# Routing tokens to expert blocks: a table written by expert and rank during attention, in place of a one-hot inversion between the stages

## The chip, the cores and the metric

The kernel runs on one core of a Trainium2 chip. The metric is the device time of one execution in microseconds; lower is better. The engines named below are TensorE (PE in the profile, with its weight loads as PEld), VectorE (DVE), ScalarE (ACT), GpSimd (POOL) and SyncE (SP). SP and POOL issue the DMAs here, each through a queue of its own, onto the same 16 DMA engines.

## The reference

Two stages follow one another. The first is attention in chunks of 64 positions; the second sends each token to one of eight experts by the cosine between the token and the expert's embedding.

```
q, k, v: (8, 8, 576, 64) fp32        # batch, heads, positions, head size
per batch, head and chunk of 64 positions:
    scores = q_c @ k_c.T / 8
    attn   = exp(scores - rowmax);  attn /= attn.sum + 1e-9
    out    = attn @ v_c
x = out as (4608, 512)               # a row is a token, all heads side by side

xn     = x / (norm(x) + 1e-6);  en = emb / (norm(emb) + 1e-6)      # emb (8, 512)
logits = xn @ en.T / tau
e      = argmax(logits)              # the first one, where two are equal
gate   = softmax(logits)[e]
y      = gate * (relu(x @ w1[e]) @ w2[e])     # w1 (8, 512, 1024), w2 (8, 1024, 512)
```

## The kernel before

**Attention.** The 4608 tokens are 36 tiles of 128. A loop over `t` runs all steps of the stage in a staggered order that is written out by hand: in one turn `turn_a(t)`, `turn_qk(t + 3)`, the loads of a later tile, `logits(t - 2)`, `scores(t + 2)`, `turn_x(t - 1)`, `values(t)`, `weights(t + 2)` and `norm(t)`. Each engine takes its instructions in the order of the program text. Loads of q, k and v go through SP's queue (L110, L123). q and k have four buffers each and v has two. `values` writes a tile of x to the DRAM tensor `x_rows` through POOL's queue (L208), from one of three SBUF buffers. `norm` sums the squares of each row on ScalarE (L213). `logits` leaves eight numbers per token in PSUM (L227); they are not yet divided by the row's norm, which changes neither the order of the experts nor their argmax.

Behind the loads of the last tiles SP's queue carries the first experts' weights (L78): for expert 0 and for expert 7, two copies of w1 and one of w2, 2 MB each. A second copy of w2 comes when the SBUF of attention is free.

**The seam.** All routing is done between the stages, for all 36 tiles at once, at L286 to L485. VectorE finds each token's expert as a one-hot row `eq`. Two matmuls with a matrix of ones and a triangular one give each token's rank among the tokens of its expert. Each expert's tokens are cut into groups of 64 (G). Step `j` of the expert stage takes two groups at a time: group `j` counted from the front, with one set of weight buffers, and group `j` counted from the back, with the other. So a block is 128 rows for two experts, there are at most 40 (`NST`), and 37 are used with these inputs. `mid` is the number of blocks.

Each token thus knows its block and its row in it. The expert stage needs the reverse: for each block and row, the token. The kernel inverts the map with one-hot matrices: for each of the 36 tiles VectorE builds a 128 x 128 matrix `oh` of rows (L470), and TensorE multiplies it with columns of token number and gate per block, summed over the tiles in `inv` (L471). `src_row`, `dst_row` and `gate_at` are read from the sum (L481 to L485). The gates themselves are computed for all tokens at once with one Sqrt and one Exp (L445, L450).

**The expert stage.** `gather(j)` fetches the 128 rows of block `j` from `x_rows` by an indirect DMA on POOL's queue (L535). `turn_xb` transposes them (L549, copied by VectorE at L551). `hidden` is the first product (L561; relu on VectorE at L572 and on ScalarE at L570), `turn_h` transposes its result (L582; copies at L586 on VectorE and L584 on ScalarE), and `result` is the second product (L594). ScalarE multiplies by the gate (L602), and an indirect DMA on POOL's queue scatters the rows to the output (L603). Weights are loaded on SP's queue under a condition, only where a block's expert differs from the one two blocks before (L522). The loop over the first 36 blocks runs, per turn, `hidden(j+1)`, `turn_h(j)`, `turn_xb(j+2)`, `result(j-1)` and `gather(j+4)`. Blocks from 36 on run under a condition, one step after the other.

Of the kernel before, what the change touches and what calls it, by code (L numbers as in the profile page):

```python
# [21 lines left out]
NO_ROW = 200000.0  # L22
# [3 lines left out]
def kernel(  # L26
# [23 lines left out]
    scale = 1.0 / float(Dh) ** 0.5  # L50

    x_rows = nc.dram_tensor("x_rows", (N, D), FP32, kind="Internal").ap()

# [9 lines left out]
    lg = keep.tile([P, NT, E], FP32, name="lg")  # L63
    nsq = keep.tile([P, NT], FP32, name="nsq")
    src_row = keep.tile([P, NST], I32, name="src_row")
    dst_row = keep.tile([P, NST], I32, name="dst_row")
    gate_at = keep.tile([P, NST], FP32, name="gate_at")
    eblk = keep.tile([1, 2, NST], I32, name="eblk")
    fresh = keep.tile([1, 2, NST], I32, name="fresh")
    n_steps = keep.tile([1, 1], I32, name="n_steps")  # L70

# [10 lines left out]

    VW = 72
    with (
# [9 lines left out]
        lg_ps = ps_l.tile([P, NT, E], FP32, name="lg_ps")  # L94
# [4 lines left out]
        enT = one.tile([P, KD, E], FP32, name="enT")  # L99

# [110 lines left out]
        def norm(t):  # L211
            junk = one.tile([P, D], FP32, tag="junk", name="junk")
            nc.scalar.activation(junk, st[t]["x"], AF.Square, accum_out=nsq[:, t : t + 1])  # L213

# [9 lines left out]
        def logits(t):  # L224
            d = st.pop(t)
            for c in range(KD):
                nc.tensor.matmul(  # L227
                    lg_ps[:, t],
                    lhsT=d["xT"][:, c],
                    rhs=enT[:, c],  # L230
                    start=(c == 0),
                    stop=(c == KD - 1),
                )

# [22 lines left out]
        for t in range(-3, NT + 2):  # L257
# [11 lines left out]
            if 0 <= t - 2:  # L269
                logits(t - 2)  # L270
            if 0 <= t + 2 < NT:
                scores(t + 2)
            if 0 <= t - 1 < NT:
                turn_x(t - 1)
# [7 lines left out]
            if 0 <= t < NT:  # L282
                norm(t)
            if t == -2:
                set_up_experts()
        nc.vector.tensor_copy(lg, lg_ps)  # L286
# [10 lines left out]

    with (  # L300
        tc.tile_pool(name="seam", bufs=1) as sp,
        tc.tile_pool(name="hot", bufs=4) as hp,
        tc.tile_pool(name="ps_r", bufs=1, space=PSUM) as ps_r,
    ):
        onesb = sp.tile([P, P], BF16, name="onesb")
        sltb = sp.tile([P, P], BF16, name="sltb")
        io_i = sp.tile([P, P], I32, name="io_i")
        io = sp.tile([P, P], FP32, name="io")
        tok_i = sp.tile([P, NT], I32, name="tok_i")
        tok1 = sp.tile([P, NT], FP32, name="tok1")  # L310
        pref = sp.tile([P, E], FP32, name="pref")
        carry = sp.tile([P, E, NT], FP32, name="carry")
        nc.vector.memset(onesb, 1.0)
        make_upper_triangular(nc, sltb, val=1.0, diag=False)
        nc.gpsimd.iota(io_i, pattern=[[1, P]], base=0, channel_multiplier=0)
        nc.gpsimd.iota(tok_i, pattern=[[P, NT]], base=1, channel_multiplier=1)
        nc.vector.tensor_copy(io, io_i)
        nc.vector.tensor_copy(tok1, tok_i)
        nc.vector.tensor_scalar(pref, io[:, 0:E], -1.0, float(E), ALU.mult, ALU.add)
        nc.vector.memset(carry, 1.0)  # L320
        nc.vector.memset(carry[:, :, 0:1], 0.0)

        ES = [P, E, NT]
        SE = [P, NT, E]

        def by_e(ap):
            return ap.unsqueeze(2).to_broadcast(ES)

        def by_s(ap):
            return ap.unsqueeze(1).to_broadcast(ES)  # L330


        lmax = sp.tile([P, NT], FP32, name="lmax")
        sel = sp.tile(ES, FP32, name="sel")
        pm = sp.tile([P, NT], FP32, name="pm")
        eq = sp.tile(ES, FP32, name="eq")
        nc.vector.tensor_reduce(lmax, lg, axis=AX.X, op=ALU.max)
        nc.vector.tensor_tensor(sel, lg.rearrange("p s e -> p e s"), by_s(lmax), ALU.is_equal)
        nc.vector.tensor_tensor(sel, sel, by_e(pref), ALU.mult)
        nc.vector.tensor_reduce(pm, sel.rearrange("p e s -> p s e"), axis=AX.X, op=ALU.max)  # L340
        nc.vector.tensor_tensor(eq, sel, by_s(pm), ALU.is_equal)


        cum = sp.tile(ES, FP32, name="cum")
        eqb = sp.tile(ES, BF16, name="eqb")
        exb = sp.tile(ES, BF16, name="exb")
        totb = sp.tile([P, E], BF16, name="totb")
        nc.vector.tensor_tensor_scan(
            cum.rearrange("p e s -> p (e s)"),
            carry.rearrange("p e s -> p (e s)"),  # L350
            eq.rearrange("p e s -> p (e s)"),
            0.0,
            ALU.mult,
            ALU.add,
        )
        nc.vector.tensor_copy(eqb, eq)
        nc.vector.tensor_tensor(exb, cum, eq, ALU.subtract)
        nc.vector.tensor_copy(totb, cum[:, :, NT - 1])
        tot = ps_r.tile([P, E], FP32, name="tot")
        rank = ps_r.tile(ES, FP32, name="rank")  # L360
        nc.tensor.matmul(tot, lhsT=onesb, rhs=totb, start=True, stop=True)
        rank_f = rank.rearrange("p e s -> p (e s)")
        nc.tensor.matmul(
            rank_f, lhsT=onesb, rhs=exb.rearrange("p e s -> p (e s)"), start=True, stop=False
        )
        nc.tensor.matmul(
            rank_f, lhsT=sltb, rhs=eqb.rearrange("p e s -> p (e s)"), start=False, stop=True
        )


        nb = sp.tile([P, E], FP32, name="nb")
        first = sp.tile([P, E], FP32, name="first")
        off = sp.tile([P, E], FP32, name="off")
        ngm1 = sp.tile([P, 1], FP32, name="ngm1")
        mid = sp.tile([P, 1], FP32, name="mid")
        half = 0.5 - 0.5 / G
        nc.vector.tensor_scalar(nb, tot, 1.0 / G, half, ALU.mult, ALU.add)
        nc.vector.tensor_scalar(nb, nb, ROUND, ROUND, ALU.add, ALU.subtract)
        nc.vector.tensor_tensor_scan(first, carry[:, 0, 1 : E + 1], nb, 0.0, ALU.mult, ALU.add)
        nc.vector.tensor_scalar(ngm1, first[:, E - 1 : E], -1.0, None, ALU.add)  # L380
        nc.vector.tensor_scalar(mid, first[:, E - 1 : E], 0.5, 0.25, ALU.mult, ALU.add)
        nc.vector.tensor_scalar(mid, mid, ROUND, ROUND, ALU.add, ALU.subtract)
        nc.vector.tensor_tensor(first, first, nb, ALU.subtract)
        nc.vector.tensor_scalar(off, first, float(G), None, ALU.mult)


        JE = [1, 2 * NST, E]
        e_of = sp.tile([1, 2, NST], FP32, name="e_of")
        jj = sp.tile([1, 2, NST], FP32, name="jj")
        ge = sp.tile(JE, FP32, name="ge")  # L390
        nc.vector.tensor_copy(jj[:, 0], io[0:1, 0:NST])
# [294 lines left out]
```

## Time and profile before

| | |
|---|---|
| median of 3 runs | 822.38 us (820.01 to 822.48) |
| the profiled execution | 820.02 us, of which the span is 818.2 us |
| TensorE busy | 749.4 us, 92% of the span |
| VectorE busy | 217.9 us, 27% |
| ScalarE busy | 181.6 us, 22% |
| GpSimd busy | 101.9 us, 12% |
| DMA | 129.99 MB in 148726 packets, 115366 of them under 512 B |
| attention | start to the last logits at 183.0 us |
| seam | to the first transposes of the expert stage at 229.5 us |
| expert stage | 15.34 us per block in the loop, to the end |

The page cuts the span into 40 slices and gives the busy share of each engine in tenths; a 9 is 90% or more. PEclk is the granted clock of TensorE, in tenths. In a timeline each line has the start and the length in microseconds, the engine, the line of the program, the operation, what it writes and reads, and in brackets how long the engine had been idle and what ended that. "Chain" means the work that ended last, followed back from the end, at each step to what released it. Times "to landing" run from the issue of a DMA until its data have arrived.

### The profile page before, as it was taken

To read this page: it belongs to the slowest core of one execution; us is meant where nothing else is said; L and a number is where in the kernel's file an instruction comes from. 1 tells how busy PE (TensorE), PEld (TensorE's weight loads), DVE (VectorE), ACT (ScalarE), POOL (GpSimd) and SP (SyncE) were. 2 spreads that over 40 slices of the span, in tenths; PEclk is the share of its full clock that TensorE was granted. 3 is DMA by queue.
4 is the path that set the end of the run, shared out by engine and by line. 5 is a ranking of instruction groups with operands and counts; after the bars stand their busy time and mean duration, and the time that the engine had idled before them with its cause. 6 is when DMAs were issued, how large, how long until landed. Compare 5 with 4: busy or idle time off the path is not lost.

```text
span 818.2 us, 14809 instructions
## 1 busy us (share of the span) xinstructions
PE 749.4 (92%) x6059; PEld 375.7 (46%) x6059; DVE 217.9 (27%) x430; ACT 181.6 (22%) x337; POOL 101.9 (12%) x133
## 2 busy tenths in 40 slices
PE   4799989980779999999999999999999999999993
PEld 3699979970723333333333333333333343343330
DVE  2577756747711111111111111111111111111110
ACT  3477755751001110110110110110110110110110
POOL 1011111110020100100100100100100100100110
PEclk9899988995579999999999999999999999999997
DMA  9999999999120100116483415788520433403140
GB/s 188 216 227 239 237 245 222 264 407 390 56 65 1 43 33 26 44 41 223 168 323 130 147 55 232 254 329 318 173 110 26 148 135 130 146 34 126 51 146 8
DMA packets 148726, 129.99 MB, mean 159 GB/s; under 512 B 115366, under 2 KB 115366, under 8 KB 148656
## 3 DMA queue, kind: packets, MB, share of 16 engines
q1 hardware_dynamic: 139552, 99.63, 42.5%
q0 software_dynamic: 9104, 29.38, 10.3%
q8 instruction: 50, 0.82, 0.4%
q14 instruction: 20, 0.16, 0.1%
HBM read 382.75 MB, written 19.14 MB: 491 GB/s over the span
## 4 chain that ended last, share of the span: by engine, by line
PE 86%; DMA 6%; DVE 3%; issue 2%; SPq 1%; ACT 1%; POOL 0%; POOLq 0%
PE y_ps L594 31%; PE h_ps L561 30%; PE ht_ps L582 5%; PE tr L134 4%; DMA w<-in_moe_w_dram 3%; PE lg_ps L227 3%; PE sc L150 3%; PE pv L190 2%; PE tr L176 2%; PE tr L219 2%; DMA qx<-in_q_dram 2%; PE x_ps L549 2%; PE inv L471 2%; DMA xin<-x_rows,src_row 0%; SPq L78 0%
## 5 line engine op out<-in xcount | busy, mean ns | idle before, releaser
L561 PE MATMUL h_ps<-w,xbT 128*64 128x512 f32 x1184 | 262.2, 595 | 3.1 <-DVE xbT L551 3.1
L594 PE MATMUL y_ps<-w,hT 128*64 128x512 f32 x1184 | 262.0, 595 | 0.0
L561 PEld LDWEIGHTS h_ps<-w,xbT 128*64 128x64 f32 x1184 | 85.0, 138 | 172.3 <-issue 168.0
L594 PEld LDWEIGHTS y_ps<-w,hT 128*64 128x64 f32 x1184 | 81.8, 137 | 154.6 <-issue 154.3
L572 DVE TENSOR_SCALAR h<-h_ps 128x512 f32<-128x512 f32 x37 | 25.6, 692 | 341.0 <-PE h_ps L561 341.0
L603 POOL DMA_INDIRECT out_dram<-y,dst_row x37 | 37.5, 1013 | 490.1 <-ACT y L602 474.1
L602 ACT ACTIVATE y<-y_ps,gate_at 128x512 f32<-128x512 f32 x37 | 25.4, 688 | 251.8 <-PE y_ps L594 245.2
L570 ACT ACTIVATE h<-h_ps 128x512 f32<-128x512 f32 x37 | 22.1, 598 | 266.6 <-PE h_ps L561 266.6
L586 DVE COPY hT<-ht_ps 128x512 f32<-128x512 f32 x37 | 25.6, 692 | 126.7 <-PE ht_ps L582 123.3
L535 POOL DMA_INDIRECT xin<-x_rows,src_row x40 | 40.9, 1021 | 50.0 <-DVE dst_row L485 38.1
L582 PEld LDWEIGHTS ht_ps<-ident,h 128*128 128x128 f32 x296 | 31.7, 141 | 30.4 <-issue 30.0
L582 PE MATMUL ht_ps<-ident,h 128*128 128x128 f32 x296 | 40.7, 280 | 0.1
L208 POOL DMA_DIRECT2D x_rows<-x x36 | 19.5, 542 | 156.7 <-DVE x L201 156.7
L227 PEld LDWEIGHTS lg_ps<-enT,xT 128*128 128x128 f32 x288 | 36.9, 201 | 1.1 <-ACT xT L221 1.1
L227 PE MATMUL lg_ps<-enT,xT 128*128 128x8 f32 x288 | 36.4, 253 | 0.7 <-ACT xT L221 0.7
L134 PE MATMUL tr<-ident,kx 128*128 128x128 f32 x144 | 24.6, 299 | 10.8 <-DMA kx<-in_k_dram 10.7
L551 DVE COPY xbT<-x_ps 128x512 f32<-128x512 f32 x37 | 25.6, 692 | 27.5 <-PE x_ps L549 23.5
L158 DVE TENSOR_REDUCE mx<-sc 128x8 f32<-128x512 f32 x36 | 24.9, 692 | 26.6 <-PE sc L150 26.6
L139 DVE COPY qxT<-tr 128x512 f32<-128x512 f32 x36 | 24.9, 692 | 25.4 <-PE tr L134 23.5
L471 PE MATMUL inv<-rr,oh 128*128 128x80 f32 x72 | 15.7, 422 | 15.1 <-DVE oh L470 15.1
L549 PE MATMUL x_ps<-ident,xin 128*128 128x128 f32 x148 | 22.8, 278 | 5.3 <-DMA xin<-x_rows,src_row 5.3
L213 ACT ACTIVATE junk<-x 128x512 f32<-128x512 f32 x36 | 22.7, 630 | 21.9 <-DVE x L201 21.9
(121 smaller groups left out, 494.2 us busy)
## 6 DMA issues: line engine op xcount, KB each, us to landing
w<-in_moe_w_dram SPq DMA_DIRECT2D x164, 2048.0 KB
v<-in_v_dram SPq DMA_DIRECT2D x64, 144.0 KB
x_rows<-x POOLq DMA_DIRECT2D x36, 256.0 KB, 4.4
kx<-in_k_dram SPq DMA_DIRECT2D x32, 256.0 KB
qx<-in_q_dram SPq DMA_DIRECT2D x32, 256.0 KB
kx<-in_k_dram SPq DMA_DIRECT2D x8, 128.0 KB
qx<-in_q_dram SPq DMA_DIRECT2D x8, 128.0 KB
xin<-x_rows,src_row POOLq DMA_INDIRECT x40, 3.6
```

What stands on the lines that cost most here:

```text
L134: nc.tensor.transpose(ps[:, i], a[:, i * P : i * P + P], ident)
L227: nc.tensor.matmul(lg_ps[:, t], lhsT=d["xT"][:, c], rhs=enT[:, c], start=(c == 0), stop=(c == KD - 1),)
L471: nc.tensor.matmul(inv.rearrange("p t k -> p (t k)"), lhsT=oh, rhs=rr[:, s].rearrange("p t k -> p (t k)"), start=(s == 0), stop=(s == NT - 1),
L535: nc.gpsimd.indirect_dma_start(out=t, out_offset=None, in_=x_rows, in_offset=bass.IndirectOffsetOnAxis(ap=src_row[:, j : j + 1], axis=0), ...
L549: nc.tensor.transpose(ps[:, c], t[:, c * P : c * P + P], ident)
L551: nc.vector.tensor_copy(xT, ps)
L561: nc.tensor.matmul(ps[G * s : G * s + G], lhsT=d["xT"][:, c, G * s : G * s + G], rhs=w1_sb[s][j % 2][:, c, fh * 512 : fh * 512 + 512], sta ...
L572: nc.vector.tensor_scalar(dst, ps, 0.0, None, ALU.max)
L582: nc.tensor.transpose(ps[:, c], d["h"][:, f0 : f0 + P], ident)
L586: nc.vector.tensor_copy(hT[:, 4 * g : 4 * g + 4], ps)
L594: nc.tensor.matmul(ps[G * s : G * s + G], lhsT=d["hT"][:, c, G * s : G * s + G], rhs=w2_sb[s][j % 2][:, c], start=(c == 0), stop=(c == KF ...
L603: ins = nc.gpsimd.indirect_dma_start(out=out, out_offset=bass.IndirectOffsetOnAxis(ap=dst_row[:, j : j + 1], axis=0), in_=y, in_offset=Non ...
```

## The change

The attention loop now also routes, in batches of four tiles (the last two have three tiles and one tile). `pick(b)` comes two turns after the batch's last tile, directly after that tile's logits; `place(b)` one turn later, between `scores` and `turn_x`. They find each token's expert and its rank among all earlier tokens of this expert, and write a record of 64 B per token (eight logits and eight copies of the token's number) to the DRAM table `spots`, at row expert x 4608 + rank. The table has 36992 rows; `clear_spots` fills all of it beforehand with a number that is no row, from SP's queue in turn `t == 0`, in pieces of 17 records (FB).

After the last batch, `groups` and `places` compute for each block and row the place in the table (four blocks first, the rest later). `groups` is ten small VectorE operations on the totals per expert; `places` is eleven for a stretch of blocks, and writes `src_row` (the place to read), `eblk` (the block's expert) and `fresh` (whether its weights must be loaded). `constants` holds some twenty small operations on GpSimd. The totals in the last `place` are two more matmuls. The expert stage reads a block in two indirect DMAs: `gather_spot` fetches the records, `gather_x` the rows of `x_rows` that they name. The output is scattered by the number in the record. The gate of each block's tokens is computed in the expert stage, by `gates(j)`, from the record's logits and the gathered rows. `norm` in attention and the seam's code from L286 to L485 are gone.

```diff
-NO_ROW = 200000.0
+NO_ROW = 200000
+    MW = 16
+    SPARE = E * N
+    FOLD = SPARE // P + 1
+    spots = nc.dram_tensor("spots", (P * FOLD, MW), FP32, kind="Internal").ap()
+    xin_sb = [keep.tile([P, D], FP32, name=f"xin{i}") for i in range(XBUF)]
+    spot = keep.tile([P, NST, MW], FP32, name="spot")
+    RB = 4
+    sizes = [RB] * (NT // RB - 1) + [RB - 1, 1]
-        lg_ps = ps_l.tile([P, NT, E], FP32, name="lg_ps")
+        rt_ps = ps_l.tile([P, 3, RB, E], FP32, name="rt_ps")
+        def constants():
...
+            nc.gpsimd.memset(empty.bitcast(I32), NO_ROW)
...
+            for x in xin_sb:
+                nc.gpsimd.memset(x, 0.0)
+        def clear_spots():
+            nc.sync.dma_start(
+                out=spots.rearrange("(p a b) m -> p a (b m)", p=P, b=FB),
+                in_=empty.rearrange("p b m -> p (b m)")
+                .unsqueeze(1)
+                .to_broadcast([P, FOLD // FB, FB * MW]),
+            )
-        def norm(t):
-            junk = one.tile([P, D], FP32, tag="junk", name="junk")
-            nc.scalar.activation(junk, st[t]["x"], AF.Square, accum_out=nsq[:, t : t + 1])
         def logits(t):
-                    lg_ps[:, t],
+                    rt_ps[:, 0, batch_of[t][1]],
+        def pick(b):
...
+            nc.gpsimd.tensor_copy(
+                m[:, 0:n, E:MW].bitcast(I32),
+                tok_i[:, t : t + n].unsqueeze(2).to_broadcast([P, n, MW - E]),
+            )
+            nc.vector.tensor_copy(lg, rt_ps[:, 0, 0:n])
+            nc.vector.tensor_reduce(lmax, lg, axis=AX.X, op=ALU.max)
+            nc.vector.tensor_tensor(sel, lg, lmax.unsqueeze(2).to_broadcast(NE), ALU.is_equal)
+            nc.vector.tensor_tensor(sel, sel, pref.unsqueeze(1).to_broadcast(NE), ALU.mult)
+            nc.vector.tensor_reduce(pm, sel, axis=AX.X, op=ALU.max)
+            nc.vector.tensor_tensor(
+                eqb[:, t : t + n], sel, pm.unsqueeze(2).to_broadcast(NE), ALU.is_equal
+            )
+            if t:
+                    nc.vector.tensor_reduce(
+                        before, eqb[:, 0:t].rearrange("p s e -> p e s"), axis=AX.X, op=ALU.add
+                    )
+        def place(b):
...
+            nc.tensor.matmul(rank, lhsT=sltb, rhs=eqb[:, t : t + n], start=True, stop=last == 0)
+            if t:
+                before = st.pop(("before", b))
+                nc.tensor.matmul(
+                    rank,
+                    lhsT=onesb,
+                    rhs=before.unsqueeze(1).to_broadcast(NE),
+                    start=False,
+                    stop=n == 1,
+                )
+            for i in range(n - 1):
+                nc.tensor.matmul(
+                    rank[:, i + 1 : n],
+                    lhsT=onesb,
+                    rhs=eqb[:, t + i].unsqueeze(1).to_broadcast([P, n - 1 - i, E]),
+                    start=False,
+                    stop=i == n - 2,
+                )
+            if b == len(sizes) - 1:
+                tot = rt_ps[:, 2, 0]
...
+            nc.vector.tensor_tensor(w, rank, e_base.unsqueeze(1).to_broadcast(NE), ALU.add)
+            nc.vector.tensor_tensor(w, w, eqb[:, t : t + n], ALU.mult)
+                nc.vector.tensor_reduce(dest[:, 0:n], w, axis=AX.X, op=ALU.add)
+            for i in range(n):
+                ins = nc.gpsimd.indirect_dma_start(
+                    out=spots,
+                    out_offset=bass.IndirectOffsetOnAxis(ap=dest[:, i : i + 1], axis=0),
+                    in_=m[:, i],
...
+        def groups():
...
+        def places(j0, j1):
...
-        for t in range(-3, NT + 2):
+        constants()
+        for t in range(-3, NT + 3):
...
             if 0 <= t + 2 < NT:
                 scores(t + 2)
+            if t - 3 in ends:
+                place(ends[t - 3])
             if 0 <= t - 1 < NT:
                 turn_x(t - 1)
...
-            if 0 <= t < NT:
-                norm(t)
+            if t - 2 in ends:
+                pick(ends[t - 2])
...
+            if t == 0:
+                clear_spots()
-        nc.vector.tensor_copy(lg, lg_ps)
+        groups()
+        places(0, XBUF)
+        def gather_spot(j):
+            gather(spot[:, j], spots, src_row[:, j : j + 1], P * FOLD)
+        def gather_x(j):
+            xin[j] = xin_sb[j % XBUF]
+            gather(xin[j], x_rows, spot[:, j, E : E + 1].bitcast(I32), N)
+        for j in range(XBUF):
+            gather_spot(j)
+        for j in range(XBUF):
+            gather_x(j)
+        places(XBUF, NST)
+        nc.vector.tensor_copy(n_steps, mid[0:1])
...
+        def gates(j):
...
+            nc.scalar.activation(junk, x, AF.Square, accum_out=rn)
+            nc.scalar.activation(rn, rn, AF.Sqrt)
+            nc.vector.tensor_reduce(lmax, lg, axis=AX.X, op=ALU.max)
+            nc.vector.tensor_scalar(rn, rn, 1e-6, None, ALU.add)
+            nc.vector.reciprocal(rn, rn)
+            nc.vector.tensor_scalar(sh, lg, lmax, rn, ALU.subtract, ALU.mult)
+            nc.scalar.activation(sh, sh, AF.Exp, accum_out=gate)
+            nc.vector.tensor_scalar(gate, gate, 1e-9, None, ALU.add)
+            nc.vector.reciprocal(gate, gate)
-            nc.scalar.activation(y, ps, AF.Copy, scale=gate_at[:, j : j + 1])
+            nc.scalar.activation(y, ps, AF.Copy, scale=d["gate"])
         turn_xb(0)
         hidden(0)
         load_w1(2)
+        gates(0)
         turn_xb(1)
+        gates(1)
+        gather_spot(XBUF)
         for j in range(LEAST + 1):
...
             if j + 2 < LEAST:
                 turn_xb(j + 2)
+                gates(j + 2)
...
             if j + XBUF < NST:
-                gather(j + XBUF)
+                gather_x(j + XBUF)
+                if j + XBUF + 1 < NST:
+                    gather_spot(j + XBUF + 1)
...
                 turn_h(j)
+                gates(j)
                 result(j)
```

## The prediction

> **What bounds the kernel now.** I read the page first, then the busy time by stretches, the chain of waits in order of time, the timeline of three places, and the landing times of the DMAs.
>
> ```profile
> span 818.2 us, 14809 instructions
> ...
> PE   4799989980779999999999999999999999999993
> ...
> PEclk9899988995579999999999999999999999999997
> DMA  9999999999120100116483415788520433403140
> ```
>
> TensorE is full in two long stretches with a hole between (a slice is 20.5 us). In the hole the granted clock falls to half; until it ends, the DMA engines are full too. By stretches (columns: stretch, its length, busy time of PE, PEld, DVE, ACT, POOL, clock, DMA share, GB/s):
>
> ```profile
> 46.00:66.00 20.00, 20.00 (x424) 18.45 (x424) 14.85 (x30) 14.04 (x31) 3.04 (x7) 1.00 1.05 236
> ...
> 183.00:195.00 12.00, 0.68 (x4) 0.24 (x3) 7.20 (x27) 2.80 (x3) 0.80 (x4) 0.50 1.04 396
> 195.00:206.00 11.00, 0.00 (x0) 0.00 (x0) 9.91 (x30) 0.44 (x1) 0.00 (x0) 0.50 1.05 387
> 206.00:225.00 19.00, 15.65 (x72) 15.43 (x72) 13.00 (x43) 0.00 (x0) 0.00 (x0) 0.50 0.08 31
> ```
>
> Attention costs 4.10 us a tile with no idle TensorE, beside a full DMA. The seam has almost no matmul, then the 72 of the inversion at half clock. The expert stage repeats every 15.34 us, TensorE full. The chain in order of time (start, length, what) says who holds the seam:
>
> ```profile
> 114.17 5.90 DMA qx<-in_q_dram
> ...
> 161.93 24.57 DMA w<-in_moe_w_dram
> ...
> 208.55 15.66 PE inv L471 x72
> 225.88 3.46 DMA xin<-x_rows,src_row
> 229.48 1.10 PE x_ps L549 x4
> ```
>
> The last logits end at 183.0 (call it T0), and the first expert transposes start at 229.48: a seam of 46.5 us. The row at 114.17 says that attention is once held by a load that came late; it also says that DMA has little to give there.
>
> **Part 1, the seam, removed and rebuilt.** All DVE rows from L286 to L485, the 36 pairs of one-hot and matmul and the direct gather go. What stands behind the last logits afterwards is a chain with three DMAs one after another:
> - Routing. Small DVE operations in the seam start 0.15 to 0.2 apart (L377 to L384), a reduction of 288 takes 0.64 (L425), a small bf16 matmul 0.17 (L361). At T0: batch 8's ranks on TensorE (0.6) and its three DVE operations (0.7), then batch 9's pick (six small, one reduction over 35 tiles: 1.9), its ranks and totals (0.6) and three DVE operations (0.8): T0+4.6.
> - Scatter. POOL takes 1.3 from one indirect DMA to the next (rows at 225.88, 227.29, 228.62). Batch 8's three start at T0+1.9 and hold the queue until T0+5.8; batch 9's starts there. Who waits for that: only the gathers behind it. The 21 DVE operations of the block table (about 4.5) are done by T0+9.1 and hide under the scatter.
> - Landing. Quiet, a row scatter lands in 2.8 and a row gather in 3.5. Under the weight loads the row writes of attention took 6.3, against 4.4 over the whole run:
>
> ```profile
> DMA to landing us min/median/max: 5.9/6.3/7.0
> ...
> x_rows<-x POOLq DMA_DIRECT2D x36, 256.0 KB, 4.4
> ...
> out_dram<-y,dst_row POOLq DMA_INDIRECT x37, 2.8
> ```
>
> The first line is x_rows between 170 and 186. The weights keep DMA full until 206 before, and later after, so I add 2 to each hop: scatter 4.8 (T0+10.6), POOL's start 0.6, first spot gather 5.5 (T0+16.7; the other three issues end at 16.4), row gather 0.5 + 5.5: T0+22.7. Bounds: quiet hops give T0+17, hops of +3.5 give T0+27. Gain: 46.5 - 22.8 = 23.7 (19 to 29).
>
> **Part 2, attention, added.** Ten batches. Per batch TensorE gets five small bf16 matmuls. They have no row in a packed sequence; nearest is the logits matmul, eight in 0.96, so 0.1 each, 0.5. DVE gets ten operations, 2.3; it has 1.0 to 1.1 idle in a tile of 4.10, so it catches up within the batch. One wait is new: the next batch's first logits overwrite what the pick reads.
>
> ```profile
> 63.15 0.69 DVE L201 TENSOR_TENSOR x<-pv,rs 128x512 f32<-128x512 f32 x1
> ...
> 63.70 0.96 PE L227 MATMUL lg_ps<-enT,xT 128*128 128x8 f32 x8
> ...
> 63.90 0.69 DVE L139 COPY qxT<-tr 128x512 f32<-128x512 f32 x1
> ```
>
> The pick starts when the x row ends, 63.84, its copy ends near 64.05, the logits wanted 63.70: 0.4 of TensorE, with scores, x transposes and values queued behind. Behind it on DVE the qxT copy (63.90) starts 1.7 to 2 late, for the six operations after the copy; the scores that need it come one tile, 4.1, later. So 0.9 a batch (0.5 to 1.5). Dropping the squares (L213) frees ACT, which is not late: nothing. On POOL four scatters (5.2) go ahead of one x_rows write; x has three buffers, 12.3 us, against 5 + 5: no stall.
>
> DMA is the dearer side. Clearing the table is 2.37 MB on SP's queue, ahead of later q, k and v loads. At the weights' 390 GB/s it takes 6.1, at attention's 236 it takes 10.0; I take 8. SP's queue idles about 4.5 between 40.4 and 46.1, so the loads behind it are 3.5 late when the full stretch begins; the first of them (tile 8) is wanted only near 50, and SP reaches it some 8 after 32.7. The scatters are 4608 rows of 64 B. Small packets: q1's 42.5% of 16 x 818.2 is 5564 engine-us, less 71.3 MB of weights at 24.4 GB/s per engine (2925), over 115366 packets: 23 ns. 4608 at 23 ns over 16 engines is 6.6 us, at nothing 0; I take 3.3, of which 20 of 36 tiles (1.8) lie before the late load. That load is then 5.3 later. It governs there: TensorE's own additions by then, 3.6, disappear in the stall. Behind it four batches at 0.9 remain: 3.6. Sum +8.9 (3.4 to 15). The last q load is issued at 156.64, lands some 5 later and is wanted at 165: with 3.5 + 3.3 against 3.5 of slack and 7 of later TensorE it does not govern again. The weights start as much later as the loads do, about 7; the first 8 MB are there by 186, before anything in the seam asks for them.
>
> The trace has no write below 512 B. The Trainium skill, in "DMA: Bandwidth & Descriptors", Specifications, says that below 512 B an engine reads, changes and writes back: a rule against this change. Doubling a packet by it would make the sum of scatters 13 instead of 3.3 and the total some 5 worse, by estimate from that page.
>
> **Part 3, the gates in the expert stage.** Each block gains a Square (0.63 + 0.19), two table loads, Sqrt, Exp and six DVE operations:
>
> ```profile
> 186.83 1.28 ACT L445 ACT_TABLE_LOAD   x1 [5.75 <-DMA w<-in_moe_w_dram]
> 188.12 0.23 ACT L445 ACTIVATE rn<-nsq 128x36 f32<-128x36 f32 x1
> ...
> 240.27 0.60 ACT L570 ACTIVATE h<-h_ps 128x512 f32<-128x512 f32 x1 [37.86 <-PE h_ps L561]
> 240.68 0.69 DVE L551 COPY xbT<-x_ps 128x512 f32<-128x512 f32 x1 [3.31 <-PE x_ps L549]
> 241.43 7.09 PE L561 MATMUL h_ps<-w,xbT 128*64 128x512 f32 x32 [0.78 <-DVE xbT L551]
> ```
>
> 0.82 + 1.28 + 0.23 + 1.28 (DVE's three beside it) + 0.45 + two DVE steps 0.5: 4.6. In the steady loop it stands between the hT copies and the next relu, beside the 7.02 of result(j-1) on TensorE, and the y copy behind it has two PSUM buffers: 0, and even with the cover gone only what exceeds some 10 us. In the conditional last block it ends near 802.3, before y at 804.25: 0. But at the start gates(0) stands ahead of the copy of xT(1) on DVE, and its ACT part behind the relu that ends at 240.87. The copy moves from 240.68 to 245.4, hidden(1) with it: +4.7 (0 if DVE runs free of ACT, 7 at most). The spot gathers add a 1.3 issue per block on POOL, which idles 490 there: 0. The constants, some twenty POOL operations and four buffer clears, lie before POOL's first x_rows write at 24.42, for which it idles 21.4: 0. The half clock of hidden(0) (8.71 instead of 7.09) stays, as the shorter seam is still an idle one.
>
> The table load row is followed by its activation at once, 1.28 later. "ScalarE: Activation LUTs", What ACT_TABLE_LOAD costs, adds a drain of 1.38 to each switch; by it the start would cost 7.5 instead of 4.7, by estimate, and the loop still nothing.
>
> **Sum.** 820.02 (span 818.2 and 1.8 around it) - 23.7 + 8.9 + 4.7 = 809.9. The median of the three runs stands 2.4 above the profiled execution; I give 810.
>
> **Rivals.**
> - *Attention takes it for nothing.* DMA's pieces at their low ends, hops quiet: +3.4 - 29 + 4.7 = -21, 799. For it: the 4.5 idle of SP's queue and the 5.9 stall that can absorb. Against it: DMA share above 1.0 in every stretch to 206. 0.24.
> - *Scatters choke the loads* (slower). If a 64 B write costs p per engine, DMA governs up to the last q tile: attention +3.5 + 288p - 4 + 1.5 (p in us, 288 packets per engine). It cancels -23.7 + 4.7 at 288p = 18, that is p = 62 ns, 2.7 times a 256 B load. At 90 ns: +27, 828. For it: full DMA, no such write in the trace. Against it: 64 B is a quarter of the bytes that take 23 ns, and the scatters are only 4608 packets beside 115366. 0.20.
> - *The gates hold every step.* If their ACT part delayed the relu by 1 a block, 36 blocks give +36, net 846. It decides from a length above some 10 us against 4.6. 0.05.
> - *The seam's DMA chain is no shorter in effect*: hops near 10 under load and attention +12 leave -2 to +2, 820. 0.08.
>
> **How the numbers follow.** Forecast 0.43 (804 to 816), rivals 0.24, 0.20, 0.05, 0.08. A difference within 0.3% (2.5 us) is about what a measurement of this kernel cannot tell from none. Faster 0.43 + 0.24 = 0.67, same 0.08, slower 0.25. The range runs from below the free attention (797) to the choked one at 90 ns (828); left out are the held gates and the tails.
>
> **What would show it.** Right: last logits near 192, first expert transposes some 23 later, no inv rows, hidden(1) held about 5 by the xbT copy, steps of 15.34 unchanged. Wrong: attention beyond 200 with longer waits for qx and kx (choked DMA); spot gathers landing above 8; steps longer than 15.4.

## The result and the profile after

The changed kernel takes 850.04 us (median of 4 runs, 849.41 to 851.02) against 822.36 for the kernel before: a ratio of 1.0345, 95% interval 1.0323 to 1.0367. It is slower; the forecast was 810, with a range to 828. The profiled execution took 849.44. From its page, the lines that answer to those of before (a slice is now 21.2 us):

```profile
span 847.3 us, 15307 instructions
...
PE   5789999889816999999999999999999999999994
...
PEclk9898776789657999999999999999999999999997
DMA  9999577789952011011566433679731253411340
```

The hole of the seam has shrunk to little more than one slice. But attention now lasts eleven slices instead of nine, the clock falls within it, and the DMA share falls to 5 to 8 tenths where it was full: attention is longer, and its loads no longer fill the DMA engines. The busy time by stretches (columns as before: stretch, length, PE, PEld, DVE, ACT, POOL, clock, DMA share, GB/s):

```profile
46.00:66.00 20.00, 17.76 (x283) 15.37 (x281) 11.76 (x31) 8.20 (x15) 6.68 (x10) 0.86 1.05 239
104.00:112.00 8.00, 6.08 (x87) 5.16 (x85) 2.94 (x7) 1.63 (x4) 4.59 (x5) 0.76 0.78 186
235.44:255.33 19.89, 0.48 (x8) 0.27 (x5) 9.52 (x47) 0.00 (x0) 11.03 (x12) 0.50 0.54 196
```

In 46 to 66 TensorE gets through 283 matmuls where it got through 424. The second row is one place where it loses time, the third the seam. For comparison, an undisturbed turn of the kernel before: the reduction of the scores starts 0.08 us after their matmuls end.

```profile
76.86 0.69 PE L150 MATMUL sc<-kxT,qxT 64*64 64x64 f32 x32
...
77.63 0.69 DVE L158 TENSOR_REDUCE mx<-sc 128x8 f32<-128x512 f32 x1 [0.76 <-PE sc L150]
```

The timeline of the place in the changed kernel, on all engines but the loads (start, length, engine, line; in brackets the idle time before and what ended it; "remote" is a release for which the trace shows no sender at that time):

```profile
104.61 1.04 POOL L363 DMA_INDIRECT spots<-m,dest  x1 [3.57 <-issue]
...
105.27 0.69 PE L213 MATMUL sc<-kxT,qxT 64*64 64x64 f32 x32
105.90 0.66 PE L278 MATMUL tr<-ident,x 128*128 128x128 f32 x4
...
106.48 0.52 PE L253 MATMUL pv<-v,aT 64*64 64x65 f32 x8
...
107.37 0.37 PE L253 MATMUL pv<-v,aT 64*64 64x65 f32 x4 [0.37 <-issue]
108.13 0.51 PE L253 MATMUL pv<-v,aT 64*64 64x65 f32 x4 [0.39 <-issue]
108.55 0.99 POOL L363 DMA_INDIRECT spots<-m,dest  x1 [0.30 <-issue]
...
110.37 0.69 DVE L221 TENSOR_REDUCE mx<-sc 128x8 f32<-128x512 f32 x1 [4.88 <-remote]
110.48 0.59 ACT L280 COPY xT<-tr 128x512 f32<-128x512 f32 x1 [5.55 <-remote]
110.94 1.11 PE L239 MATMUL tr<-ident,a 128*128 128x128 f32 x4
```

The scores end at 105.96 and the x transposes at 106.56, yet the reduction and the copy that need only these start at 110.37 and 110.48, shortly after the fourth scatter's row has ended at 109.54. Meanwhile TensorE gets four or five small pv matmuls every 0.72 us, where 32 take 0.70 in an undisturbed turn. Behind the stall the same four transposes take 1.11 instead of 0.66: the granted clock is 0.50 from 110.9 to 113.4. Two turns of the loop then take about 9.2 and 6.3 us instead of 4.09 each, and this comes back at each of the batches of four tiles whose scatters find scores still to come, seven in all.

The seam, in the chain of work that ended last (start, length, what):

```profile
239.59 0.98 POOL spots L363
...
241.05 4.79 DMA spots<-m,dest
...
246.72 0.35 POOL spot L509
...
252.04 3.25 DMA xin<-x_rows,spot
255.33 1.13 PE x_ps L583 x4
```

The last logits end at 235.44 (183.0 before) and the first expert transposes start at 255.33: the seam is 19.9 us instead of 46.5. In the expert stage the forecast's wait is there, and after it the steps are 15.34 again:

```profile
269.56 1.28 ACT L602 ACT_TABLE_LOAD   x1
...
271.45 0.67 DVE L585 COPY xbT<-x_ps 128x512 f32<-128x512 f32 x1
...
272.18 3.52 PE L614 MATMUL h_ps<-w,xbT 128*64 128x512 f32 x8 [4.97 <-DVE xbT L585]
```

Attention gives +52.4, the seam -26.6, the start of the expert stage +4.2 (a wait of 4.97 where it was 0.78), +0.6 (hidden(0) 9.29 instead of 8.71) and +1.6 (hidden(1) 8.67 instead of 7.09, at a granted clock of 0.81 instead of 1.00). The end, from the last transposes of hidden rows on, is 3.3 shorter (19.4 instead of 22.7; why, no run shows). Together that is +28.9, and the spans differ by 29.1. What the forecast missed lies in attention: +52.4 instead of +8.9.

### The profile page after: what moved, and what is told of

It reads as the page before. It is cut to its first block, busy times and chain, and to the rows that moved or that the text cites. A ratio compares the mean times of both kernels' runs of the same rounds, so it can differ in the third digit from the quotient of the medians.

```text
span 847.3 us, 15307 instructions
## 1 busy us (share of the span) xinstructions
PE 776.2 (92%) x6031; PEld 392.5 (46%) x6031; DVE 248.5 (29%) x687; ACT 290.3 (34%) x520; POOL 186.1 (22%) x238
## 4 chain that ended last, share of the span: by engine, by line
PE 85%; issue 5%; DVE 3%; DMA 3%; ACT 1%; POOL 1%; SPq 0%; DVEq 0%; POOLq 0%; ACTq 0%
PE y_ps L647 30%; PE h_ps L614 30%; PE ht_ps L635 4%; PE pv L253 4%; PE rt_ps L286 4%; PE tr L197 3%; PE sc L213 3%; DMA qx<-in_q_dram 2%; PE tr L278 2%; PE tr L239 2%; PE x_ps L583 2%; DVE mx L221 1%; DVE a L223 1%; DMA spots<-m,dest 1%; POOL spot L509 0%
## 5 line engine op out<-in xcount | busy, mean ns | idle before, releaser
L656 POOL DMA_INDIRECT out_dram<-y,spot x37 | 37.9, 1024 | 438.4 <-ACT y L655 409.3
L655 ACT ACTIVATE y<-y_ps,gate 128x512 f32<-128x512 f32 x37 | 25.4, 687 | 126.1 <-PE y_ps L647 126.1
L280 ACT COPY xT<-tr 128x512 f32<-128x512 f32 x36 | 21.1, 587 | 111.8 <-PE tr L278 71.6
L253 PE MATMUL pv<-v,aT 64*64 64x65 f32 x1152 | 42.4, 258 | 14.5 <-issue 13.7
L286 PEld LDWEIGHTS rt_ps<-enT,xT 128*128 128x128 f32 x288 | 44.1, 234 | 4.7 <-DVE m L308 2.2
L509 POOL DMA_INDIRECT xin<-x_rows,spot x40 | 41.3, 1032 | 21.9 <-issue 11.9
L286 PE MATMUL rt_ps<-enT,xT 128*128 128x8 f32 x288 | 43.6, 278 | 2.3 <-ACT aT L241 1.0
L363 POOL DMA_INDIRECT spots<-m,dest x36 | 36.1, 1003 | 40.9 <-issue 40.0
L509 POOL DMA_INDIRECT spot<-spots,src_row x40 | 40.4, 1010 | 16.5 <-issue 11.9
L253 PEld LDWEIGHTS pv<-v,aT 64*64 64x64 f32 x1152 | 31.3, 160 | 26.7 <-issue 26.4
```

The costliest lines, as they stand in the source:

```text
L253: nc.tensor.matmul(pv[CH * c : CH * c + CH, par, i], lhsT=d["aT"][r0 : r0 + CH, i, CH * c : CH * c + CH], rhs=v_t[b][r0 : r0 + CH, i, cb, ...
L286: nc.tensor.matmul(rt_ps[:, 0, batch_of[t][1]], lhsT=d["xT"][:, c], rhs=enT[:, c], start=(c == 0), stop=(c == KD - 1),)
L363: ins = nc.gpsimd.indirect_dma_start(out=spots, out_offset=bass.IndirectOffsetOnAxis(ap=dest[:, i : i + 1], axis=0), in_=m[:, i], in_offse ...
L509: nc.gpsimd.indirect_dma_start(out=dst, out_offset=None, in_=table, in_offset=bass.IndirectOffsetOnAxis(ap=at, axis=0), bounds_check=rows - 1,
L656: ins = nc.gpsimd.indirect_dma_start(out=out, out_offset=bass.IndirectOffsetOnAxis(ap=spot[:, j, E : E + 1].bitcast(I32), axis=0), in_=y, ...
```

## The experiments

The measure that I use throughout is the time from the end of the scores on TensorE to the start of the mx reduction on VectorE. It is 0.07 us at the median in the kernel before, and never above 0.1 there. In the changed kernel it is 3.1 to 4.7 in seven turns. I call this excess the delay, or the hold. Each kernel's time stands beside that of the kernel before on the same chip. Down to `lean` each time and each trace is that of a single execution; the end of attention differs by 2.5 us between two traces of one kernel (`spread` and `spread2`). Turns are counted from the logits' starts.

**What is it: the scatters, or the pick and place that go with them?**

`late`: all 36 scatters after the loop, with ten buffers for records and ranks. `scatter()` issues the first of those that wait.

```diff
-            for i in range(n):
-                ins = nc.gpsimd.indirect_dma_start(
...
+            waiting.extend((m[:, i], dest[:, i : i + 1]) for i in range(n))
...
+        while waiting:
+            scatter()
         groups()
```

> All 36 scatters are issued after the attention loop; pick and place stay in it. In the changed kernel the last logits are at 235.4 us, against 183.0 before, and in eight batches TensorE's values and the two engines that wait for it stand some 5 us while POOL issues four scatters. Theory A (the scatters, as POOL issues them, hold TensorE): the stalls go, last logits near 190 (183 + 8 batches x 0.9), while the seam grows by about 36 x 1.3 = 47 us, so the whole stays within 10 us of 850. Theory B (the ten small operations of pick and place and their waits hold it): the stalls of 5 us stay and the last logits stay at 225 to 240; the whole is near 890.

840.63 us (818.82 before). The last logits end at 191.6, and no reduction waits above 0.32 us. The 36 scatters in the seam make it 53.8 long instead. So pick, place and the clearing of the table cost attention 8.6, and the scatters where they stood cost the other 43.8. In its full stretch a batch costs two turns of 4.32 instead of 4.09, 0.45 us. The rest is mostly a balance of waits for loads: the turns of 8.16 and 7.44 that the kernel before has from 113 to 129 are not there, two of 8.53 and 6.72 stand behind the clearing of the table, and two of 6.36 and 6.89 from 158 to 171.

`spread`: the same queue of scatters, one to a turn, behind the x_rows write.

```diff
+            if waiting:
+                scatter()
             if 0 <= t + 2 < NT:
                 weights(t + 2)
```

> One scatter a turn, behind the turn's x_rows write, instead of four in a row. In the changed kernel TensorE still ran beside the first scatter of a batch and stood from the second on. Theory A1 (each indirect issue of 1.3 us holds TensorE): 36 holds of about 1.2 us, last logits 225 to 240, the whole 840 to 855. Theory A2 (only several in a row hold it): no stall, last logits near 190, the whole near 805. Theory B (pick and place): as in the changed kernel, 850.

813.41 us (818.82 before): last logits at 193.5, first expert transposes at 218.5. The same 36 scatters cost little one at a time. So Theory A1's hold is there, but short: where a scatter falls on the end of the scores, the reduction starts 0.3 to 0.5 us after the scatter's row, and four of the 36 reductions are delayed by 1.0 to 1.3 us. The longest of them:

```profile
61.19 0.69 PE L213 MATMUL sc<-kxT,qxT 64*64 64x64 f32 x32
...
61.88 1.03 POOL L368 DMA_INDIRECT spots<-m,dest  x1 [0.30 <-issue]
...
63.20 0.69 DVE L221 TENSOR_REDUCE mx<-sc 128x8 f32<-128x512 f32 x1 [1.92 <-PE tr L278]
```

Most turns stay at 4.1 to 4.6; of the longer ones the longest, 7.03, holds a wait of 2.29 for a load of q. Signals between other engines get through: beside the scatter at 76.90 to 77.92 ScalarE's exponential starts at 77.77, 0.04 us after the end of the VectorE subtraction that it waits for.

**Is it the small writes, or the indirect issue?**

`direct`: the four scatters replaced by four plain DMAs of the same 64 B records, in the order of the tokens.

```diff
-                ins = nc.gpsimd.indirect_dma_start(
-                    out=spots,
...
+                r0 = P * (t + i)
+                nc.gpsimd.dma_start(out=spots[r0 : r0 + P, :], in_=m[:, i])
```

> The four scatters of a batch become four plain DMAs of the same 64 B rows, in the order of the tokens, on the same queue. The records then do not stand at their places, so most blocks find no rows and the expert stage fetches fewer rows of x; attention alone is read. Theory A (the indirect issue): no stall, last logits near 190. Theory C (many writes of 64 B to DRAM): the stalls of 5 us stay, last logits 225 to 240.

803.56 us (818.82 before), last logits at 188.7. Four in a row stand at 108.06, the next reduction waits for nothing:

```profile
107.79 0.69 PE L213 MATMUL sc<-kxT,qxT 64*64 64x64 f32 x32
108.06 2.12 POOL L364 DMA_DIRECT2D spots<-m  x4 [0.29 <-POOL m L301]
108.62 0.67 DVE L221 TENSOR_REDUCE mx<-sc 128x8 f32<-128x512 f32 x1
```

The same bytes on the same queue, in the trace in packets of 512 B like the scatters', do no harm; no reduction is delayed by more than 0.31. Theory C falls, and with it the rival of the forecast that small writes choke the DMA engines.

`fetch`: four indirect gathers from the table in the scatters' place; no record is written.

```diff
...
-                    out=spots,
-                    out_offset=bass.IndirectOffsetOnAxis(ap=dest[:, i : i + 1], axis=0),
-                    in_=m[:, i],
-                    in_offset=None,
+                    out=got,
+                    out_offset=None,
+                    in_=spots,
+                    in_offset=bass.IndirectOffsetOnAxis(ap=dest[:, i : i + 1], axis=0),
```

> The four scatters of a batch become four indirect gathers of 64 B rows from the cleared table into SBUF, with the same indices and on the same queue. The table gets no records, so the expert stage fetches no rows of x; attention alone is read. Theory A (any indirect issue): stalls of 5 us stay, last logits 225 to 240. Theory C (writes of 64 B to DRAM) or a cause that belongs to scatters alone: no stall, near 190.

842.51 us (818.82 before), last logits at 233.3, delays of 4.0 to 4.6. Its waits for a signal that came late (engine, what, line; total, times, longest):

```profile
ACT xT L280 <- remote: 37.1, 7, 5.6
DVE mx L221 <- remote: 32.4, 7, 4.9
```

So it isn't writing: indirect gathers do it as well.

**Does it need full DMA engines, 128 records, or a busy GpSimd?**

`quiet`: q, k and v of the first tiles used again.

```diff
...
+            if t >= 4:
+                for nm in ("kx", "qx"):
+                    qk_t[nm, t] = first_qk[nm, t % 4]
+                return
...
+            if b >= 2:
+                v_t[b] = v_t[b % 2]
+                return
```

> The changed kernel, four scatters in a row kept, with the loads of q and k left out from the fifth tile on and those of v from the third batch on: the first tiles' data are used again, so its output is not the reference's, and each core DMA engine has far less to do while attention runs. Theory D (the indirect writes hold up TensorE because they find the DMA engines' queues full): the eight stalls go, 8 x 7.6 = 61 us at most, attention becomes free of loads and its last logits come at or before 180 us. Theory P (GpSimd issuing several indirect DMAs in a row holds back TensorE's signals and its dense small matmuls, whatever the DMA engines do): the stalls of about 5 us stay, eight waits of the xT copy and of the mx reduction of 4.9 to 5.6 us each, and the last logits come at 220 to 235 us.

826.38 us (819.21 before), last logits at 212.6. Its page and its late signals:

```profile
DMA  9994111111610426626101516011526555311240
...
ACT xT L289 <- remote: 37.3, 7, 5.5
DVE mx L230 <- remote: 25.2, 7, 4.8
```

In most of attention the DMA engines are busy for 1 tenth, and the stalls remain (delays of 2.9 to 4.4). Theory D falls. The delays are mostly the shorter ones because six of the seven reductions are let go behind the third scatter of the row; the copy xT then starts 0.8 to 1.5 us after them. The last logits come earlier than Theory P's 220, partly since the first ones start at 27.1 instead of 34.6 and the turn behind a stall is often back at 4.09.

`few`: 16 of the 128 records of each scatter.

```diff
-                    out_offset=bass.IndirectOffsetOnAxis(ap=dest[:, i : i + 1], axis=0),
-                    in_=m[:, i],
+                    out_offset=bass.IndirectOffsetOnAxis(ap=dest[0:16, i : i + 1], axis=0),
+                    in_=m[0:16, i],
```

> The changed kernel, four scatters in a row kept, each of only the first 16 of the 128 token records (the others are left out, so most blocks hold no tokens and the output is not the reference's). Theory N (the hold follows the number of records that GpSimd makes descriptors for): an eighth of it is left, under 1 us per batch, and the last logits come at 190 to 196 us. Theory I (the hold belongs to each indirect issue, whatever its size): if GpSimd's rows stay near 1.0 us, the stalls stay at about 5 us and the last logits near 230 us; if its rows become shorter, the stall shrinks with them.

853.37 us (819.21 before), last logits at 241.0.

```profile
86.27 0.69 PE L213 MATMUL sc<-kxT,qxT 64*64 64x64 f32 x32
...
89.16 0.84 POOL L363 DMA_INDIRECT spots<-m,dest  x1 [0.30 <-issue]
...
91.35 0.69 DVE L221 TENSOR_REDUCE mx<-sc 128x8 f32<-128x512 f32 x1 [4.87 <-remote]
```

An eighth of the records, GpSimd rows of 0.86 at the median instead of 1.00, and delays no shorter (4.2 to 5.1): Theory I, the hold belongs to the issue. But its last clause fails: the rows became shorter and the stall did not. From the start of the first issue to that of the reduction it is 5.6 to 6.3, beside 5.7 to 5.9 in six of the seven cases of the changed kernel. The Trainium skill, "DMA: Bandwidth & Descriptors", Anatomy of one DMA, calls the making of descriptors small, so that many can be made before it shows. The rows agree; that the issue holds TensorE, it does not say.

`busy`: `late`, and four fills of 128x1024 on GpSimd where the four scatters stood.

```diff
...
+            for i in range(n):
+                nc.gpsimd.memset(idle, 0.0)
```

> All 36 scatters after the loop (as in the run that showed 840.6 us and last logits at 191.6), and in each batch, where the four scatters stood, four fills of 128x1024 on GpSimd in a row, about 1 us each by the rows of 128x512 (0.53). Theory O (any work of GpSimd's of that length beside the dense small matmuls holds TensorE, through a port or a bus that both use): the stalls of about 5 us come back, last logits near 235 us. Theory I (only the issue of indirect DMAs does): no stalls, last logits at 190 to 194 us, total 839 to 843.

845.62 us (823.57 before), 22 above its neighbour as `late` was; last logits at 192.6, no delay above 0.32.

```profile
91.14 3.99 POOL L364 MEMSET idle<- 128x1024 f32 x4
```

Four microseconds of fills on GpSimd cost attention nothing that shows (192.6 beside 191.6 in `late`). Theory O falls, for work that only writes; GpSimd work that reads was not tried.

**How does it grow, and what does it hold?**

`pairs`: two scatters in every second turn, 36 as before.

```diff
-            if waiting:
+            if waiting and t % 2:
                 scatter()
+                if waiting:
+                    scatter()
```

> The 36 scatters spread, but two in a row in every second turn in place of one in each turn (which was 813.4 us, last logits 193.5). Theory S (the hold lasts as long as GpSimd's row of indirect issues, about 1.3 us each, and a turn of 4.1 us has about 1 us of slack for it): a pair holds for 2.6 us, some 1 to 1.6 us beyond the slack, 18 times, and the clock after it is slower as well: last logits at 205 to 225 us, total 825 to 843. Theory T (a hold needs more than two in a row, for instance a queue that holds two): last logits at 193 to 196, total about 813.

832.89 us (819.21 before), last logits at 214.8: within Theory S's range. The delays above 1 us number 13 and last 1.7 to 2.7. One of them:

```profile
82.39 0.69 PE L213 MATMUL sc<-kxT,qxT 64*64 64x64 f32 x32
...
84.25 1.00 POOL L368 DMA_INDIRECT spots<-m,dest  x1 [0.30 <-issue]
...
85.64 0.69 DVE L221 TENSOR_REDUCE mx<-sc 128x8 f32<-128x512 f32 x1 [3.25 <-remote]
```

Counted from the start of the first issue, a held reduction starts after 1.3 to 1.6 us with one in a row, 2.7 to 3.2 with two, and with four in the changed kernel, `fetch` and `few` 5.6 to 6.3 (once 4.2, let go behind the third): 1.3 to 1.6 per issue, and what exceeds the slack of a turn is lost. It does not follow the length of GpSimd's rows, as `few` has shown.

`lean`: four scatters in a row, and a quarter of the pv matmuls of a tile (4 of 16 in the program; each is two rows in the trace, so 8 of the 32 there, not 4 as the expectation has it).

```diff
...
-            for i in range(NPAIR):
+            n_i = NPAIR if t < 4 else 1
+            for i in range(n_i):
```

> The changed kernel, four scatters in a row kept, with only 4 of the 32 small pv matmuls of a tile from the fifth tile on (the other 28 are left out and their results repeat the first ones, so the output is not the reference's). Theory Q (while GpSimd issues, TensorE is only short of instructions: in the stalls it gets some ten matmuls and weight loads every 0.72 us, and a tile of attention has about 200): with 56 fewer to issue in the turn of the stall, mx and xT wait 2 us less, and the stall is at most about 3 us. Theory H (TensorE's signals to the other engines are held back until GpSimd is through): the reduction mx and the copy xT still wait 4.9 to 5.7 us, seven or eight times each, though nothing dense stands behind them, and the last logits come less than 1 us a tile (some 30 us) before those of the changed kernel (235.4): at 205 to 235.

842.86 us (823.57 before), last logits at 225.5.

```profile
ACT xT L281 <- remote: 32.6, 6, 5.8
DVE mx L221 <- remote: 20.4, 4, 5.2
```

The delays are 2.5 to 5.2, five of seven above 4. With three quarters of the pv matmuls gone the signals are still held; Theory Q's limit of 3 us is broken. TensorE trickles in the same time here too; what part of the stall that makes, no run separates.

**Is it so beside other matmuls?** The trace of the change has rows of three indirect DMAs in nearly every block of the expert stage:

```profile
391.76 1.03 POOL L656 DMA_INDIRECT out_dram<-y,spot  x1 [11.66 <-ACT y L655]
...
394.20 0.69 DVE L625 TENSOR_SCALAR h<-h_ps 128x512 f32<-128x512 f32 x1 [6.18 <-PE h_ps L614]
394.43 1.01 POOL L509 DMA_INDIRECT spot<-spots,src_row  x1 [0.30 <-issue]
```

VectorE's relu falls within or just behind such a row in 33 blocks, and in each it starts 0.05 us after the matmuls that it reads. In attention nothing held by two issues was let go before 2.7 us; here it is 2.4 us after the first issue, and on time. So the hold does not come with every row of indirect DMAs: it was seen beside attention's short matmuls only. In nearly all blocks the relu stands at this same moment, just behind the second issue; other moments were not tried there.

**A version that beats both.** `spread2` is `spread` again, timed; the two others add one edit each.

> The 36 scatters one to a turn, behind the x_rows write, timed: 1 to 1.5 per cent below the kernel before (about 812 of 822 us), which the one look of it gave (813.4 beside 818.8).

812.69 us, ratio to the kernel before 0.9888 (0.9863 to 0.9913).

`gates_late`, ahead of the loop over blocks:

```diff
-        gates(0)
         turn_xb(1)
+        gates(0)
```

> As spread2, and the transposes and the copy of step 1's block stand ahead of gates(0) instead of behind them. If the forecast's Part 3 is right that gates(0) cost 4.7 us there, TensorE's wait of about 5 us before hidden(1) goes and the time falls by 4 to 5 us against spread2, to about 0.979 of the kernel before. Rival: gates(0) then come later in VectorE's and ScalarE's order, and hold the first turned blocks of hidden in their place: no gain.

804.81 us, ratio 0.981 (0.9786 to 0.9835). The first line is of `spread2`, the second of `gates_late`, both hidden(1):

```profile
235.43 4.89 PE L623 MATMUL h_ps<-w,xbT 128*64 128x512 f32 x14 [4.98 <-DVE xbT L594]
```

```profile
229.13 7.09 PE L623 MATMUL h_ps<-w,xbT 128*64 128x512 f32 x32 [0.78 <-DVE xbT L594]
```

The wait has gone, and nothing is late in its place: from the start of hidden(0) to that of hidden(1) it is 10.6 instead of 15.0, a gain of 4.3. Behind the shorter wait hidden(1) itself also runs faster, 7.0 us to the next transposes instead of 8.7, at a granted clock of 1.00 instead of 0.80: another 1.7. These 6.0 stand beside 6.4 by the ratios; the medians differ by 7.9. In the two profiles attention also ends 2.3 earlier, which the edit does not touch (the one kernel `spread` and `spread2` itself differs by 2.5 there).

`third_buffer`, in `pick` and `place`:

```diff
-            m = wk.tile([P, RB, MW], FP32, tag="m", name="m")
+            m = wk.tile([P, RB, MW], FP32, tag="m", name="m", bufs=3)
...
-            dest = wk.tile([P, RB], I32, tag="dest", name="dest")
+            dest = wk.tile([P, RB], I32, tag="dest", name="dest", bufs=3)
```

> As gates_late, and a third buffer for the records m and their ranks dest, so that the last pick need not wait for the scatter of the batch before it (a wait of 4.68 us of VectorE in the seam of the one look). If that wait is what sets the seam there, the first expert transposes come 4 to 5 us earlier and the time falls by as much against gates_late. Rival: the scatters' landing behind the weight loads sets the seam, then at most 1 to 2 us.

802.03 us, ratio 0.9754 (0.9729 to 0.978): 20 us below the kernel before and 48 below the change as it was made. The wait of VectorE for the older scatter is no longer there and the seam is 23.2 instead of 27.7, as expected. The time falls by less than the expected 4 to 5: the medians differ by 2.8, as attention ends 1.9 later in this profile. The interval touches that of `gates_late` nowhere.

## Why the prediction was wrong, by its own steps

- **The step that failed** is in Part 2: "On POOL four scatters (5.2) go ahead of one x_rows write; x has three buffers, 12.3 us, against 5 + 5: no stall." It asked who is queued behind the scatters on their own engine, and was right about that queue. The only other price of the scatters was their packets (3.3 of DMA time). Neither asks what a row of indirect issues does to another engine. The trace of before had indirect DMAs only in the seam and in the expert stage, none beside attention's small matmuls, so this cost had no row; it was set to nothing where it should have been bounded from above. The runs show that such a row holds up TensorE's results. Its size: 43.8 us (`late` against the change), 5.5 for each of the eight batches of four.
- **Attention's other costs**, +8.9 (3.4 to 15): `late` shows +8.6. That the sum came out is partly luck, for its parts did not. TensorE pays 0.45 a batch rather than 0.9. Behind the clearing two turns take 8.53 and 6.72, some 7 more than 4.09 each, where 5.3 was reckoned; but the stall of the kernel before, 7.4 more than two turns, goes, and another of some 5 comes at 158 to 171.
- **Small writes**: the Trainium skill, "DMA: Bandwidth & Descriptors", Specifications, has an engine read, change and write back below 512 B, which the prediction weighed at some 5 us. `direct` shows no such price: it writes the same 64 B records, and its attention ends at 188.7. In the trace of the change the 4608 scattered records are 576 packets of 512 B, which take 17.5 us of engine time, 1.1 over 16 engines, where 3.3 was reckoned. So no run shows the 23 ns a record that this term went by.
- **The rival of choked loads** had the direction (828, slower) by a mechanism that did not happen. Its sign in the profile was to be longer waits for qx and kx and a DMA that governs; the DMA share fell instead, and `direct` and `quiet` rule it out.
- **The seam**, T0+22.7: 19.9. The scatter landed at T0+10.4 as reckoned (10.6); the last row gather took 3.25, not 5.5, as the weights had been loaded by then in the longer attention (a DMA share of 0.05 from 246 to 252). With attention short (`third_buffer`) that share is 1.05 from 201 to 207 and the seam 23.2, near the forecast.
- **The gates**: the wait before hidden(1) is 4.97, 4.2 more than before, against 4.7; `gates_late` removes it. The sum left out what the wait does to the clock: hidden(1) then takes 8.67 instead of 7.09, 1.6 more. The steps stay at 15.34, so the gates hold nothing there. A table load's activation follows it by 0.02 (269.34 after 268.04 + 1.28), without the drain that the Trainium skill, "ScalarE: Activation LUTs", What ACT_TABLE_LOAD costs, adds.

With a term of 43.8 for the scatters the forecast would have been 854, beside 850 measured. What inside the chip is held stays open: whether only the way of TensorE's signals, or TensorE's own issue as well, which trickles in the same time. So does why the expert stage, with three indirect DMAs in a row beside matmuls of 512 columns, shows no delay: it was not tried with four in a row, nor in another place of the step.

## What to carry to other kernels

An indirect DMA can have a price outside its queue and its bytes: where GpSimd issues several in a row beside short matmuls whose results other engines wait for, put them one at a time between other work, and count the slack of a turn against one issue (1.3 to 1.6 us here). When a change puts an operation next to work that it never stood next to in the trace, a cost of nothing is a guess; reckon at least with the length of the operation. Where an engine's result is ready and its reader waits for a "remote" signal, look at what all other engines were doing just then.

## What the runs showed that I had not expected

- While GpSimd issues indirect DMAs in a row in attention, TensorE's results reach VectorE and ScalarE 3.1 to 4.7 us late with four, 1.7 to 2.7 with two, up to 1.3 with one. The number of records (16 or 128), the direction, and the load of the DMA engines make little difference; four plain DMAs (2.12 us) and four fills (3.99 us) do nothing. In the expert stage, beside long matmuls, a result comes through on time (0.05 us) behind the second of three.
- The stall costs again through the clock: four transposes of 0.66 take 1.11 just behind it, at a granted clock of 0.50, and the following turn takes 6.3 instead of 4.09.
